# Crossbar transposes from chunk 12 on, later loads held behind them, and the third tile's attention moved under the first G2 tile

## The chip, the cores and the metric

One NeuronCore of a Trainium2 chip. The metric is the device time of one execution in microseconds (us). "Span" is the time from the first to the last instruction in the profile; it is some 1.7 us shorter than the time.

## The reference

Retention attention (a causal product with decay in place of a softmax) over q, k, v of 8 x 8 heads x 576 x 64, and then an expert layer with Mish over the 4608 tokens that come out:

```python
scores = scale * np.matmul(q, k.transpose(0, 1, 3, 2))
Dmat = np.where(rel >= 0, gamma[:, None, None] ** rel[None, :, :], 0.0)
attn = np.matmul(scores * Dmat[None], v)                      # [8, 8, 576, 64]
x = attn.transpose(0, 2, 1, 3).reshape(4608, 512)
h = x @ w_in                                                  # w_in 512 x 2048
g = h * np.tanh(softplus(h))                                  # Mish
out = g @ w_out                                               # w_out 2048 x 512
```

## The kernel before

The 4608 tokens are 36 chunks of 128. Four chunks are a tile of the expert layer (9 tiles); two chunks are a pair, the unit of loading. The names that the profile uses: `qks` is q and k of a pair after scaling by the decay (DVE), `qkT` the same transposed, `sc` the scores in PSUM, `hp` the product with w_in (G1), `gT` its Mish (ACT), `ops` the product with w_out (G2). PE works through one list of instructions in order: G1 and G2 blocks of four 128x512 matmuls (0.865 us each), with the attention of later chunks in between.

How a chunk or pair is transposed before the change:

```python
    NPE = 16
    def step_t(n):
        m, u = divmod(n, 2)
        r = pairs[m]
        # ... (cut: allocate r["qk"], the tile qkT)
        if n >= NPE:                       # from pair 8 on: the DMA crossbar
            nc.sync.dma_start_transpose(out=r["qk"]..., in_=r["qks"]...)
            return
        tp = ps_sc.tile([P, 4, NP, P], BF16, name="sc")[:, 0:2]
        for i in range(2):                 # q, then k: eight transposes by TensorE
            flat = r["qks"][:, i, u].rearrange("p h d -> p (h d)")
            for p in range(NP):
                nc.tensor.transpose(tp[:, i, p, :], flat[:, ts(p, P)], ident)
        if n < 2 * NCH:                    # chunks 4 to 7: two copies, after all eight
            nc.scalar.copy(r["qk"][:, 0, u], tp[:, 0])
            nc.vector.tensor_copy(r["qk"][:, 1, u], tp[:, 1])
        else:
            nc.scalar.copy(r["qk"][:, :, u], tp)
```

How loads are released. A crossbar transpose is issued on SP. GpSimd (POOL) issues the loads; its one-element copy of `qkT` makes it stand until the transpose has landed, and only then come its next loads. A load of a pair is three DMAs: q and k (512 KB each) and v (256 KB written, cast to bf16).

```python
    def cross(m):
        step_t(2 * m)
        nc.gpsimd.tensor_copy(seen, pairs[m]["qk"][0:1, 0, 0, 0, 0:1])

    # ... visit(m, 0) of pairs 4 to 6: load(m + 4), not held by anything
    #     pair 8:                      cross(8); load(11)
    #     m = 8 to 16:                 cross(m + 1); load(m + 4)
```

## Time and profile before

| kernel before | |
|---|---|
| time, median of 3 runs | 317.3 us (317.11 to 317.51) |
| span of the profiled run, granted clock | 315.3 us, 1.0 |
| PE busy | 304.6 us, 97% of the span |
| matmuls, of them in the chunk 12 to 15 transposes | 2635, 32 |
| crossbar transposes | 10, pairs 8 to 17 |
| G2 of the first tile starts | 57.71 us |
| scores of pair 8 / pair 9 start | 112.81 / 128.47 us |

The table is read from the top down: if PE is busy 97% of the span at the full clock, a change can win only by matmuls taken off PE or by waits of PE that go; and it can lose by any wait that it adds, since PE takes its list in order. The prediction below shows the rows behind this. One more line, from the list of DMA issues (count, median us from issue to landing):

```profile
qkT<-qks SPq DMA_TRANSPOSE x10, 4.4
```

### The profile page before, as it was taken

How to read it: one execution, taken by the hardware profiler on the slowest of the kernel's cores; microseconds unless marked ns; L12 is line 12 of the kernel's file. 1: busy time of each engine (PE TensorE's matmuls, PEld its weight loads, DVE VectorE, ACT ScalarE, POOL GpSimd, SP SyncE). 2: the span in 40 equal slices, each digit the busy share in tenths (PEclk: the TensorE clock that was granted, in tenths of full speed). 3: DMA queues.
4: the chain of work that ended last, by engine and by line, in shares of the span. 5: the costliest groups of instructions: out<-in, count | busy, mean ns of one | idle time of the engine just before them, and what ended most of it. 6: DMA issues, size and time to landing. Idle time of an engine off the chain costs nothing.

```text
span 315.3 us, 6082 instructions
## 1 busy us (share of the span) xinstructions
PE 304.6 (97%) x2635; PEld 158.8 (50%) x2635; DVE 134.9 (43%) x182; ACT 127.2 (40%) x212; POOL 78.7 (25%) x102
## 2 busy tenths in 40 slices
PE   6889999999999999999999999999999999999995
PEld 2455588655455554444545454445454545444444
DVE  5743574247738482626262626262626232001011
ACT  5667566324355542343434343434343432333300
POOL 6586672543340223122403040320000000000000
PEclk9999999999999999999999999999999999999999
DMA  6999999999996395969595969694040401000032
GB/s 171 261 178 223 197 208 221 201 228 246 221 238 79 78 199 113 189 102 197 131 174 116 185 127 175 139 163 103 33 102 33 102 33 35 33 33 35 33 83 83
DMA packets 72474, 43.38 MB, mean 138 GB/s; under 512 B 55680, under 2 KB 63616, under 8 KB 72448
## 3 DMA queue, kind: packets, MB, share of 16 engines
q0 software_dynamic: 43952, 26.22, 56.2%
q1 hardware_dynamic: 28352, 16.65, 21.3%
q8 instruction: 20, 0.33, 0.5%
q10 hardware_dynamic: 144, 0.13, 0.1%
q14 instruction: 6, 0.05, 0.0%
HBM read 36.70 MB, written 9.44 MB: 146 GB/s over the span
## 4 chain that ended last, share of the span: by engine, by line
PE 89%; DVE 3%; SPq 2%; DMA 2%; ACT 2%; issue 1%; DVEq 0%
PE hp L385 34%; PE ops L423 33%; PE hp L423 6%; PE hp L408 4%; PE sc L321 3%; PE sc L370 2%; PE sc L363 2%; SPq L137 2%; PE st L342 2%; DMA kraw<-in_k_dram 2%; PE sc L296 1%; PE hp L435 1%; DVE sm L324 1%; PE hp L396 1%; ACT qkT L298 0%
## 5 line engine op out<-in xcount | busy, mean ns | idle before, releaser
L385 PE MATMUL hp<-xT,w_in_t 128*128 128x512 bf16 x496 | 126.6, 380 | 0.7 <-ACT gT L387 0.7
L387 ACT ACTIVATE gT<-hp 128x512 bf16<-128x512 f32 x124 | 74.2, 599 | 128.5 <-PE hp L385 128.3
L423 PE MATMUL ops<-w_out_t,gT 128*128 128x512 bf16 x480 | 121.9, 379 | 0.2 <-DVE res L443 0.2
L423 PEld LDWEIGHTS <-gT 128*128 128x128 bf16 x560 | 54.2, 98 | 65.1 <-issue 1.3
L443 DVE COPY res<-ops 128x512 f32<-128x512 f32 x30 | 20.8, 692 | 129.0 <-PE ops L423 129.0
L385 PEld LDWEIGHTS <-w_in_t 128*128 128x128 bf16 x496 | 46.0, 98 | 53.8 <-issue 1.2
L324 DVE TENSOR_TENSOR sm<-sc,mask 128x1024 bf16<-128x1024 f32 x36 | 42.7, 1218 | 13.9 <-PE sc L321 13.9
L568 POOL COPY seen<-qkT 1x1 bf16<-1x1 bf16 x10 | 1.8, 178 | 128.2 <-DMA qkT<-qks 128.2
L346 ACT ACTIVATE ssb<-st,diag 128x512 bf16<-128x512 f32 x32 | 20.3, 685 | 15.5 <-PE st L342 15.5
L374 DVE CAST xT<-sc 128x512 bf16<-128x512 f32 x32 | 20.8, 686 | 6.7 <-PE sc L370 5.8
L107 POOL DMA_DIRECT2D qraw<-in_q_dram x16 | 17.2, 1074 | 13.1 <-DVE qks L280 7.5
L280 DVE TENSOR_TENSOR qks<-kraw,gk 128x1024 bf16<-128x1024 f32 (+1 forms) x18 | 19.8, 1102 | 0.0
L280 DVE TENSOR_TENSOR qks<-qraw,gq 128x1024 bf16<-128x1024 f32 (+1 forms) x18 | 19.8, 1098 | 0.0
L107 POOL DMA_DIRECT2D kraw<-in_k_dram x16 | 17.1, 1070 | 10.5 <-issue 4.9
L423 PE MATMUL hp<-w_out_t,gT 128*128 128x512 bf16 x80 | 18.8, 380 | 0.0
L107 POOL DMA_DIRECT2D v<-in_v_dram x16 | 17.2, 1074 | 6.2 <-DMA kraw<-in_k_dram 2.5
L408 PE MATMUL hp<-xT,w_in_t 128*128 128x128 bf16 x272 | 16.9, 219 | 0.0
L408 PEld LDWEIGHTS <-w_in_t 128*128 128x128 bf16 x272 | 15.4, 98 | 0.7 <-issue 0.2
L370 PE MATMUL sc<-sm,v 128*64 128x128 bf16 x288 | 13.8, 220 | 0.6 <-DVE sm L324 0.6
L321 PEld LDWEIGHTS <-qkT 64*128 64x128 bf16 x288 | 8.1, 94 | 9.8 <-issue 5.9
L410 ACT ACTIVATE gT<-hp 128x512 bf16<-128x512 f32 x17 | 10.2, 598 | 7.0 <-PE hp L408 6.8
L321 PE MATMUL sc<-qkT 64*128 64x128 bf16 x288 | 11.9, 218 | 1.1 <-DVE qkT L299 0.9
(75 smaller groups left out, 153.5 us busy)
## 6 DMA issues: line engine op xcount, KB each, us to landing
out_dram<-res SPq DMA_DIRECT2D x31, 256.0 KB, 3.5
qraw<-in_q_dram POOLq DMA_DIRECT2D x12, 512.0 KB, 8.1
kraw<-in_k_dram POOLq DMA_DIRECT2D x12, 512.0 KB, 9.3
v<-in_v_dram POOLq DMA_DIRECT2D x12, 256.0 KB, 9.8
qraw<-in_q_dram POOLq DMA_DIRECT2D x8, 256.0 KB, 9.4
kraw<-in_k_dram POOLq DMA_DIRECT2D x8, 256.0 KB, 9.4
w_out_t<-in_moe_w_out_dram POOLq DMA_DIRECT2D x4, 512.0 KB, 11.6
w_in_t<-in_moe_w_in_dram POOLq DMA_DIRECT2D x6, 256.0 KB, 7.1
```

The costliest lines, as they stand in the source:

```text
L107: nc.gpsimd.dma_start(out=r[x][ds(off, ni)].rearrange("p u h d -> p (u h) d"), in_=src[ds(b, 2), :, ds(i0, ni), :].rearrange("b h p d -> p ...
L280: nc.vector.tensor_tensor(r["qks"][:, i, u], r["qk"[i]][:, u], g, op=OP.mult)
L321: nc.tensor.matmul(sc[:, e, p, :], lhsT=qk[r, 1, u, p, :], rhs=qk[r, 0, u, p, :], start=True, stop=True)
L324: nc.vector.tensor_tensor(sm.rearrange("p e n i -> p (e n) i"), sc.rearrange("p e n i -> p (e n) i"), (mask if len(chunks[n]) == 1 else ma ...
L346: nc.scalar.activation(ssb[:, :, :, e, :], st, AX.Copy, scale=diag[:, e:e + 1])
L370: nc.tensor.matmul(ot[ds(64 * e, 64), p, :], lhsT=vs[:, u, 2 * p + e, :], rhs=sm[:, e, p, :], start=(start and p == 0), stop=True, skip_gr ...
L374: (nc.scalar.copy if t == 0 else nc.vector.tensor_copy)(xts[t][:, :, ts(s, P)], ot)
L385: nc.tensor.matmul(hp, lhsT=w_in_t[:, c, ts(f, P)], rhs=xts[t][:, c, :], start=(c == 0), stop=(c == KC - 1))
L387: nc.scalar.activation(gts[t][:, f, :], hp, AX.Mish)
L408: nc.tensor.matmul(hp[:, j, :], lhsT=w_in_t[:, c, ts(f + j, P)], rhs=xts[t][:, c, ts(s, P)], start=(c == 0), stop=(c == KC - 1))
L423: nc.tensor.matmul(ops, lhsT=gts[t][:, f, ts(s, P)], rhs=w_out_t[:, f, :], start=(f == 0), stop=(f == nF - 1))
L443: copy(ot, ops)
```

## The change

Its intent: take the 32 transposes of chunks 12 to 15 off PE by using the crossbar from pair 6 on; hold the loads of pairs 8 to 11 until the transposes ahead of them have landed, so that the two do not meet; put the attention of the third tile (pairs 4 and 5) evenly under the first G2 tile; let the q and k copies of a chunk start earlier. The core of the diff, cut (allocation moved into `turned`, xT copies of chunks 4 to 11 moved from DVE to ACT, and the start, are left out):

```diff
-    NPE = 16
 def step_t(n):                                      # chunks 4 to 7
-        for i in range(2):
+        for i, copy in enumerate((nc.scalar.copy, nc.vector.tensor_copy)):
             for p in range(NP):
                 nc.tensor.transpose(tp[:, i, p, :], flat[:, ts(p, P)], ident)
-        nc.scalar.copy(r["qk"][:, 0, u], tp[:, 0])
-        nc.vector.tensor_copy(r["qk"][:, 1, u], tp[:, 1])
+            copy(qk[:, i, u], tp[:, i])             # between the two halves
+def turn_pair(m, i):                                # pairs 4 and 5: q half, k half
+        if "tp" not in r:
+            r["tp"] = ps_sc.tile([P, 2, 2, NP, P], BF16, name="sc")   # one tile for both
+        ... eight transposes into r["tp"][:, i], then nc.scalar.copy(qk[:, i], tp)
     # first G2 tile:  turn_pair, scores, output of pairs 4 and 5 at i = 2 ... 13
     for i in range(8):                              # second G2 tile, first half
+        elif i == 2:
+            cross(6)
+            load(8)
     for i in range(nF):                             # G1 of tile 2 with the rest of G2
+        elif i == 6:
+            cross(7)
+            load(9)
-        elif i == 11:
+        elif i == 14:
             cross(8)
+            load(10)
             load(11)
```

More of the change, by code (lines that the diff above doesn't have):

```diff
@@ L280, in step_p, with turned @@
             nc.vector.tensor_tensor(r["qks"][:, i, u], r["qk"[i]][:, u], g, op=OP.mult)
-    def step_t(n):
-        m, u = divmod(n, 2)
+    def turned(m):
         r = pairs[m]
@@ L287, in step_t, with cross @@
             r["qk"] = tr.tile([P, 2, 2, NP, P], BF16, name="qkT", bufs=3)
-        if n >= NPE:
-            nc.sync.dma_start_transpose(out=r["qk"].rearrange("p i u n t -> p (i u n) t"),
-                                        in_=r["qks"].rearrange("p i u h d -> p (i u h d)"))
-            return
-        tp = ps_sc.tile([P, 4, NP, P], BF16, name="sc")[:, 0:2]
-        for i in range(2):
+        return r["qk"]
+    def step_t(n):
+        m, u = divmod(n, 2)
+        qk = turned(m)
+        tp = ps_sc.tile([P, 4, NP, P], BF16, name="sc")
+        for i, copy in enumerate((nc.scalar.copy, nc.vector.tensor_copy)):
+            flat = pairs[m]["qks"][:, i, u].rearrange("p h d -> p (h d)")
+            for p in range(NP):
+                nc.tensor.transpose(tp[:, i, p, :], flat[:, ts(p, P)], ident)
+            copy(qk[:, i, u], tp[:, i])
+    def turn_pair(m, i):
+        r = pairs[m]
+        qk = turned(m)
+        if "tp" not in r:
+            r["tp"] = ps_sc.tile([P, 2, 2, NP, P], BF16, name="sc")
+        tp = r["tp"][:, i]
+        for u in range(2):
             flat = r["qks"][:, i, u].rearrange("p h d -> p (h d)")
             for p in range(NP):
-                nc.tensor.transpose(tp[:, i, p, :], flat[:, ts(p, P)], ident)
-        if n < 2 * NCH:
-            nc.scalar.copy(r["qk"][:, 0, u], tp[:, 0])
-            nc.vector.tensor_copy(r["qk"][:, 1, u], tp[:, 1])
-        else:
-            nc.scalar.copy(r["qk"][:, :, u], tp)
+                nc.tensor.transpose(tp[:, u, p, :], flat[:, ts(p, P)], ident)
+        nc.scalar.copy(qk[:, i], tp)
+    def cross(m):
+        r = pairs[m]
+        qk = turned(m)
+        nc.sync.dma_start_transpose(out=qk.rearrange("p i u n t -> p (i u n) t"),
+                                    in_=r["qks"].rearrange("p i u h d -> p (i u h d)"))
+        nc.gpsimd.tensor_copy(seen, qk[0:1, 0, 0, 0, 0:1])
     def step_n(m):
@@ L373, in step_o @@
             xts[t] = xp.tile([P, KC, NCH * P], BF16, name="xT")
-        (nc.scalar.copy if t == 0 else nc.vector.tensor_copy)(xts[t][:, :, ts(s, P)], ot)
+        (nc.scalar.copy if t < 3 else nc.vector.tensor_copy)(xts[t][:, :, ts(s, P)], ot)
     gts = {}
@@ L503 @@
     first(2, "O")
-    first(3, "kQK")
-    for f in range(4):
+    first(3, "kQ")
+    steps = {0: "K", 1: "S", 3: "O"}
+    for f in range(5):
         g1_some(0, f, NCH - 1)
-        first(3, {0: "S", 2: "O"}.get(f, ""))
+        first(3, steps.get(f, ""))
     g1_chunk(3, 0)
-    for i in range(4, nF):
-        if i == 5:
+    g1_chunk(3, 4, 1)
+    for i in range(5, nF):
+        if i == 6:
             step_n(0)
-        elif i == 7:
+        elif i == 8:
             step_k(0)
         elif i == 9:
+            one(4, "P")
+        elif i == 10:
             step_n(1)
-        elif i == 12:
-            one(4, "PT")
+        elif i == 11:
+            one(4, "T")
+        elif i == 13:
+            one(4, "S")
         elif i == 14:
-            one(4, "S")
             one(5, "P")
@@ L541, with scores, output @@
     load(7)
-    def visit(m, w):
-        n = 2 * m
-        if w == 0:
-            if 2 * m + 2 < NPE:
-                load(m + 4)
-        elif w == 2:
-            if m == 5:
-                step_k(1)
-            one(n, "T")
-        elif w == 3:
-            one(n + 1, "T")
-        elif w == 5:
-            one(n, "S")
-            one(n + 1, "S")
-        elif w == 7:
-            step_k(m)
-            one(n, "O")
-            one(n + 1, "O")
-            if 2 * m + 2 < NPE:
-                step_p(m + 1)
-    def cross(m):
-        step_t(2 * m)
-        nc.gpsimd.tensor_copy(seen, pairs[m]["qk"][0:1, 0, 0, 0, 0:1])
+    def scores(m):
+        one(2 * m, "S")
+        one(2 * m + 1, "S")
+    def output(m):
+        step_k(m)
+        one(2 * m, "O")
+        one(2 * m + 1, "O")
     for i in range(nF):
-        if i == 6:
+        if i == 0:
             step_p(4)
-        elif i >= 8:
-            visit(4, i % 8)
+        elif i in (2, 10):
+            turn_pair(4 + i // 8, 0)
+        elif i in (3, 11):
+            turn_pair(4 + i // 8, 1)
+        elif i in (5, 13):
+            scores(4 + i // 8)
+        elif i == 8:
+            output(4)
+            step_p(5)
+        elif i == 12:
+            step_k(1)
         g2(0, i)
     for i in range(8):
-        visit(5, i)
+        if i == 0:
+            output(5)
+            step_p(6)
+        elif i == 2:
+            cross(6)
+            load(8)
         g2(1, i)
     for i in range(nF):
-        visit(6 + i // 8, i % 8)
-        if i == 9:
+        if i == 2:
+            scores(6)
+            step_p(7)
+        elif i == 5:
+            output(6)
+        elif i == 6:
+            cross(7)
+            load(9)
+        elif i == 10:
+            scores(7)
             step_p(8)
-        elif i == 11:
+        elif i == 13:
+            output(7)
+        elif i == 14:
             cross(8)
+            load(10)
             load(11)
@@ L594 @@
             m, w = 2 * (t + 1) + i // 8, i % 8
-            n = 2 * m
             if m < n_pairs:
                 if w == 0:
-                    one(n, "S")
-                    one(n + 1, "S")
+                    scores(m)
                     if m + 1 < n_pairs:
@@ L606 @@
                 elif w == 4:
-                    step_k(m)
-                    one(n, "O")
-                    one(n + 1, "O")
+                    output(m)
             if t < nT:
```

## The prediction

> **What bounds the kernel now.** I read the page's busy table first, then the waits of PE, then the timelines of PE, ACT, DVE and SP around the parts that the change touches.
>
> ```profile
> PE 304.6 (97%) x2635; PEld 158.8 (50%) x2635; DVE 134.9 (43%) x182; ACT 127.2 (40%) x212; POOL 78.7 (25%) x102
> PEclk9999999999999999999999999999999999999999
> DMA  6999999999996395969595969694040401000032
> ```
>
> PE is busy 304.6 of 315.3 us at the full clock; nothing else is over 43%. So only two things move the end: matmuls taken off PE, and PE's idle time. The DMA row matters too: the 16 DMA engines are saturated over the first 13 slices, to about 97 us. The waits of PE name the idle time that can be had:
>
> ```profile
> PE sc L321 <- DVE qkT L299: 0.9, 3, 0.3
> PE sc L262 <- ACT qkT L265: 0.8, 1, 0.8
> PE hp L385 <- ACT gT L387: 0.7, 1, 0.7
> PE sc L363 <- DVE sm L324: 0.3, 1, 0.3
> PE ops L423 <- DVE res L443: 0.2, 1, 0.2
> ```
>
> That is 2.9 us in all; the rest of the idle time lies in the first 17 us, which the change leaves alone. The second line deserves a look: four q transposes of chunk 3, then four k transposes into the same PSUM tile, and in between ACT's copy of the q half must end. The stretch of chunk 5 and that of pair 4 (chunks 8 and 9) show what transposes cost where they do not wait so (timelines of PE, then ACT, then DVE):
>
> ```profile
> 36.94 0.61 PE L296 MATMUL sc<-ident,qks 128*128 128x128 bf16 x8
> 37.38 1.06 PE L408 MATMUL hp<-xT,w_in_t 128*128 128x128 bf16 x16
> 38.73 0.40 PE L321 MATMUL sc<-qkT 64*128 64x128 bf16 x8 [0.28 <-DVE qkT L299]
> 66.35 0.61 PE L296 MATMUL sc<-ident,qks 128*128 128x128 bf16 x8
> 66.79 1.03 PE L423 MATMUL ops<-w_out_t,gT 128*128 128x512 bf16 x4
> 67.66 0.61 PE L296 MATMUL sc<-ident,qks 128*128 128x128 bf16 x8
> ...
> 37.14 0.60 ACT L387 ACTIVATE gT<-hp 128x512 bf16<-128x512 f32 x1 [1.36 <-PE hp L385]
> 37.63 0.58 ACT L298 COPY qkT<-sc 128x512 bf16<-128x512 bf16 x1
> 67.05 1.01 ACT L301 COPY qkT<-sc 128x1024 bf16<-128x1024 bf16 x1 [8.54 <-PE sc L296]
> ...
> 38.24 0.42 DVE L299 COPY qkT<-sc 128x512 bf16<-128x512 bf16 x1 [1.00 <-ACT qkT L298]
> ```
>
> Eight transposes hold PE for 37.38 - 36.94 = 0.44 us. ACT's copy of the q half of chunk 5 starts 0.69 us after the first transpose, since a Mish of the matmuls before is still running, and ends at 1.27 us. Chunks 6 and 7 repeat this to 0.01 us.
>
> The crossbar's price, from SP's and POOL's timelines:
>
> ```profile
> 103.54 1.86 SPq L289 DMA_TRANSPOSE qkT<-qks  x1
> 107.95 0.18 POOL L568 COPY seen<-qkT 1x1 bf16<-1x1 bf16 x1 [18.06 <-DMA qkT<-qks]
> ```
>
> Issued at 103.54, landed by 107.95: 4.4 us on quiet DMA engines, no PE time, and PE uses the result only at 112.8, so it is hidden.
>
> **What the Trainium skill says.** "TensorE: Matmul & The Clock Gate", in "Wait — 56ns, not 53.3ns?", gives 55.6 ns from one warm 128-column matmul to the next; the trace agrees, 0.44 us for eight. "PSUM — Partial Sum Buffer", in "Terms", says that TensorE writing and ScalarE reading the same bank and quadrant at once is an error. The q and k halves of the new step_t are 1 KiB each and share a 2 KiB bank, so they have to be serialised; the chunk 3 wait above is such a wait in this trace. "DMA: Bandwidth & Descriptors", in "Issuing engines are not separate DMA queues", says that DMAs from all issuing engines share the 16 DMA engines and interleave. The trace agrees: output stores of 256 KB land 7.8 to 8.9 us after issue while loads saturate the engines, 2.0 us when alone.
>
> **The change part by part.** I compared the two built programs engine by engine, with the instruction that each semaphore wait stands for.
>
> *Transposes of chunks 12 to 15 go to the crossbar.* 32 matmuls fewer, four groups of 0.44 us, all in the saturated stretch: -1.8 us.
>
> *Waits that go.* The output step of chunk 4 now stands two g1 blocks behind its scores instead of one: -0.35. The scores of chunks 5 to 7 waited 0.28 to 0.30 each for DVE's copy; PE will arrive later (next part), so these go: -0.9. The 0.69 before g1 of tile 2 goes, because the attention now ends eight g2 groups earlier, and about 0.15 comes back from a PSUM buffer that a store must free: -0.55. The 0.25 behind a late store goes: -0.25. Sum -2.05.
>
> *step_t, rewritten.* The old one ran all eight transposes and then both copies. The new one runs four, then ACT's copy, then four, then DVE's copy, in one PSUM tile. In the built program the fifth transpose of each of chunks 4 to 7 waits for exactly ACT's copy of the first four. By chunk 5's numbers that copy ends at 1.27 us, the fifth transpose starts about 1.32 us after the first, and would have started at 0.22: PE stands 1.10 us. PE works in order, so nothing fills it. Four chunks: +4.4.
>
> *turn_pair.* The k half of pairs 4 and 5 waits for ACT's copy of the q half in the same tile. The copy ends 0.70 + 1.01 = 1.71 us after the first transpose, so k can start at about 1.76; PE gets there after eight transposes and a g2 group, 67.66 - 66.35 = 1.31. Two pairs of 0.45: +0.9.
>
> *Start.* g1 of block 0 fills the wait between chunk 3's q and k transposes, and a fifth block is done before chunk 3 joins. But the 128-column block that completes it is only 0.23 us long, so the next g1 meets a PSUM buffer whose Mish is not done, some 0.6 us. Walking both orders through with the durations shown I get +0.2 for the new one.
>
> *Later loads held.* Pair 8's load waits for pair 6's transpose, pair 9's for pair 7's, and those of 10 and 11 for pair 8's. PE's old waits show no loads to wait for, so this costs only where a transpose is late. Pair 6: transposed after load 7 is in, slack about 3 us. Pair 7: DVE scales it some 5.1 us after the scores of pair 6 start (0.5 + two masks 2.3 + two scalings 2.3), the transpose overlaps the end of load 8, and the scores are due 12.4 us after pair 6's: slack 1 to 2 us. Pair 8: scaled 5.1 us after the scores of pair 7, which stand only 9.8 us before its own (six g1 and three g2 groups of 0.865, output and scores 2.0). Even at 4.4 us it lands with about 0.3 us to spare, and load 9 is still running then. One transpose of this trace that met the tail of loads and a store took 5.6 us; I expect 6 to 6.5. PE then waits 1 to 2 us: +1.4, the least certain term.
>
> The xT copies of chunks 4 to 11 move from DVE to ACT (0.59 against 0.69 us); neither engine is full in that stretch, so no time.
>
> Sum: -1.8 - 2.05 + 4.4 + 0.9 + 0.2 + 1.4 = +3.05. From 317.3 this gives 320.3 us.
>
> **The rivals.** *The plain gain*: the fifth transpose does not really stand, or the time is made up by the waits behind it. Then -1.8 - 2.05 + 0.2 remains, 313.7 us. For it speaks that the change plainly aims there; against it the wait in the built program and the 0.83 us that the same pattern costs at chunk 3. *DMA contention*: the bunched loads 9, 10 and 11 delay the transposes of pairs 8 and 9. At the 8 us that stores take under saturation, pair 8 would cost 3.5 us and pair 9 up to 1 more: 323 us. Against it: load 9 is more than half done when pair 8's transpose is issued. *ACT as the new bound* in the chunk stage: a Mish of 0.60, xT and qkT copies of 0.58 each per 0.9 us block. But they fall in different blocks, and the stand of PE gives ACT time; at most 0.5 us.
>
> **Range and chances.** The four stands of step_t are the firmest term after the 1.8 us, the wait for pair 8 the loosest (0 to 3.5 us). Low end: no such wait and part of the stand made up, 316.8. High end: contention, 322.5. Faster by 2% means under 311.0, below even the plain gain: 0.01. Slower by 2% needs over 323.6: 0.05. Within 2%: 0.94.
>
> **What would show it.** Right: PE waits of about 1.1 us, four times, for ACT's qkT copy in step_t; two of about 0.45 in turn_pair; PE near 2607 matmuls and some 1.5 us less busy; 12 DMA transposes; no wait of the scores of chunks 5 to 7; one wait of 1 to 2 us of the scores of pair 8 for its transpose. Wrong: no PE wait in step_t (the plain gain), waits of several us at pairs 7, 8 and 9 (contention), or PE waiting for Mish through the chunk stage.

## The result, and the profile after

| | before | after | after - before |
|---|---|---|---|
| time, median (us) | 317.4 (317.11 to 318.74, 4 runs) | 329.25 (328.48 to 329.56, 4 runs) | +11.9 |
| ratio of fast runs | | 1.0361, 95% 1.0327 to 1.0396 | |
| span of the profiled run | 315.3 | 327.6 | +12.3 |
| G2 of the first tile starts | 57.71 | 61.62 | +3.9 |
| scores of pair 8 start | 112.81 | 117.35 | +4.5 |
| scores of pair 9 start | 128.47 | 138.35 | +9.9 |

A ratio here is the mean time of one kernel's fast runs over the mean of the other's fast runs of the same rounds, so it is not quite the ratio of the medians. The last four rows say where the loss lies: 3.9 us before the first G2 tile, 0.6 from there to pair 8, 5.3 between pair 8 and pair 9, and 2.4 after pair 9. The page of the kernel after has the rows that answer to those quoted in the prediction:

```profile
PE 306.0 (93%) x2607; PEld 158.5 (48%) x2607; DVE 130.5 (40%) x174; ACT 128.0 (39%) x217; POOL 79.5 (24%) x104
PEclk9999999999999999879999999999999999999999
DMA  6999999996599969998979797979040400000023
```

PE has 28 matmuls fewer, as it should (32 transposes gone, 4 small G1 matmuls added), and yet is busy 1.4 us longer: the clock row has an 8 and a 7, where the same work takes more time. The two costliest of PE's waits:

```profile
PE sc L337 <- DMA qkT<-qks: 8.0, 2, 5.3
PE sc L295 <- ACT qkT L296: 3.8, 4, 0.9
```

The columns after the colon are us in total, times, and the longest. L337 is the scores, L295 the transposes of step_t; two waits of 0.3 us each of turn_pair's transposes come further down. The waits on the path before (0.9 of the scores for DVE's copy, for one) are gone; in their place stand 8.0 us for crossbar transposes. One of the four step_t stands (a stand is time in which PE idles at a wait), in PE's timeline (start, us, what; idle time before it and its releaser in brackets):

```profile
31.64 0.39 PE L295 MATMUL sc<-ident,qks 128*128 128x128 bf16 x4
32.96 0.38 PE L295 MATMUL sc<-ident,qks 128*128 128x128 bf16 x4 [0.94 <-ACT qkT L296]
33.19 1.89 PE L401 MATMUL hp<-xT,w_in_t 128*128 128x512 bf16 x8
```

From the first transpose to the work behind the last one 33.19 - 31.64 = 1.55 us pass, where the kernel before needs 0.44. Now the crossbar transposes of pairs 8 and 9. SP issues them at 109.94 and at 122.61 us; POOL's copy, in POOL's timeline, runs as soon as one has landed:

```profile
117.43 0.18 POOL L317 COPY seen<-qkT 1x1 bf16<-1x1 bf16 x1 [9.33 <-DMA qkT<-qks]
138.43 0.18 POOL L317 COPY seen<-qkT 1x1 bf16<-1x1 bf16 x1 [13.40 <-DMA qkT<-qks]
```

From issue to landing pair 8's takes 7.4 us and pair 9's 15.7 us (landing at 138.30), against 4.3 to 4.4 us for those of this kernel that meet no load. The loads of pairs 10 and 11 were issued from 118.13 to 123.84 and landed from 124.08 to 139.47: pair 9's transpose stands in the middle of them. And what PE does after it:

```profile
132.05 1.03 PE L439 MATMUL ops<-w_out_t,gT 128*128 128x512 bf16 x4
138.35 1.03 PE L337 MATMUL sc<-qkT 64*128 64x128 bf16 x16 [5.28 <-DMA qkT<-qks]
139.32 1.89 PE L401 MATMUL hp<-xT,w_in_t 128*128 128x512 bf16 x4
141.00 1.91 PE L439 MATMUL ops<-w_out_t,gT 128*128 128x512 bf16 x4
142.71 1.51 PE L401 MATMUL hp<-xT,w_in_t 128*128 128x512 bf16 x4
144.05 1.03 PE L439 MATMUL ops<-w_out_t,gT 128*128 128x512 bf16 x4
```

A block of four such matmuls starts 0.865 us after the one before at the full clock; here the steps are 1.68, 1.71 and 1.34, together 2.1 us too long, and the scores themselves took 0.97 instead of 0.55. These 2.5 us are the 2.4 that the table has after pair 9, to 0.1.

**Why does a transpose take 15.7 us?** The trace keeps every DMA packet. A pair's transpose is 2048 packets of 256 B. The view of DMA packets over 128 to 131 us, and again over 134 to 137 us (queue 0 is POOL's loads, queue 1 SP's; columns: packets, MB, share of the 16 engines):

```profile
q0 software_dynamic: 171, 0.63, 97.1%
q1 hardware_dynamic: 166, 0.04, 11.6%
```

```profile
q0 software_dynamic: 1236, 0.16, 79.8%
q1 hardware_dynamic: 1236, 0.32, 79.8%
```

In the first stretch the loads are q and k, in packets of 4 KB; in the second v, in packets of 128 B. In both, the transpose gets one packet for each packet of the load: 55 per us beside q and k, 412 per us beside v, where it makes some 840 per us alone. This is what the Trainium skill says in "DMA: Bandwidth & Descriptors", "Queues, rings and completion order": an engine takes turns between its queues packet by packet. Turns of that kind favour whoever has the large packets: a 256 B packet against a 4 KB one is a sixteenth of the bytes. Two parts of the 15.7 us are not turns. The transpose's first packet came 5.3 us after its issue (1.2 us when quiet), which no run explains. And from 132 to 134 us, behind a fetch of instructions, both queues nearly stood: 329 packets of the transpose where the 412 per us above would make some 820, which is 1.2 us lost (see the last section).

### The profile page after: what moved, and what is told of

Read it like the earlier page. It is cut to its first block, busy times and chain, and to the rows that moved or that the text cites. A ratio compares the mean times of both kernels' runs of the same rounds, so it can differ in the third digit from the quotient of the medians.

```text
span 327.6 us, 6045 instructions
## 1 busy us (share of the span) xinstructions
PE 306.0 (93%) x2607; PEld 158.5 (48%) x2607; DVE 130.5 (40%) x174; ACT 128.0 (39%) x217; POOL 79.5 (24%) x104
## 4 chain that ended last, share of the span: by engine, by line
PE 82%; DMA 11%; SPq 2%; ACT 2%; DVE 1%; issue 1%; POOL 0%; ACTq 0%; POOLq 0%
PE hp L401 31%; PE ops L439 29%; DMA qkT<-qks 7%; PE hp L439 5%; PE hp L424 5%; PE sc L337 3%; DMA w_in_t<-in_moe_w_in_dram 2%; SPq L136 2%; PE sc L386 2%; PE sc L379 2%; PE st L358 2%; DMA kraw<-in_k_dram 2%; PE hp L451 1%; DVE qks L279 1%; PE sc L308 1%; ACT qkT L296 1%
## 5 line engine op out<-in xcount | busy, mean ns | idle before, releaser
L403 ACT ACTIVATE gT<-hp 128x512 bf16<-128x512 f32 x123 | 73.4, 597 | 147.3 <-PE hp L401 147.0
L337 PE MATMUL sc<-qkT 64*128 64x128 bf16 x288 | 12.3, 223 | 8.3 <-DMA qkT<-qks 8.0
L337 PEld LDWEIGHTS <-qkT 64*128 64x128 bf16 x288 | 8.4, 96 | 16.9 <-DMA qkT<-qks 9.0
L390 DVE CAST xT<-sc 128x512 bf16<-128x512 f32 x24 | 15.4, 685 | 0.9
L426 ACT ACTIVATE gT<-hp 128x512 bf16<-128x512 f32 (+1 forms) x18 | 10.3, 579 | 8.2 <-PE hp L424 7.9
```

The lines of the kernel that those rows point to most:

```text
L337: nc.tensor.matmul(sc[:, e, p, :], lhsT=qk[r, 1, u, p, :], rhs=qk[r, 0, u, p, :], start=True, stop=True)
L390: (nc.scalar.copy if t < 3 else nc.vector.tensor_copy)(xts[t][:, :, ts(s, P)], ot)
L403: nc.scalar.activation(gts[t][:, f, :], hp, AX.Mish)
```

## The experiments

All twelve gave correct results. The kernel before ran beside each on the same chip, with medians of 317.09 to 317.13 us. Each edit is against the changed kernel unless it says otherwise.

| run | what it does | expected us | measured us, median | ratio to before, 95% |
|---|---|---|---|---|
| a1 | copies of step_t after all eight | 325.7 | 324.72 | 1.0216 to 1.0301 |
| a2 | one load a transpose | 321.5 | 321.4 | 1.0089 to 1.0176 |
| a3 | pair 9's wait filled with matmuls | 326.8 | 327.13 | 1.0290 to 1.0325 |
| a4 | kernel before, step_t's copies split | 320.8 | 320.75 | 1.0098 to 1.0129 |
| b1 | a1, own tiles, loads a pair earlier | 313.5 to 315 | 318.79 | 1.0024 to 1.0084 |
| b2 | loads a pair earlier | 318.7 | 321.1 | 1.0077 to 1.0175 |
| b3 | kernel before, crossbar for pairs 6, 7, not held | 325 | 332.4 (fast runs) | 1.0391 to 1.0518 |
| b4 | v of pairs 10, 11 before q and k | 321.5 | 338.82 | 1.0647 to 1.0722 |
| c1 | new order, pairs 6, 7 on TensorE | 315.3 | 315.61 | 0.9943 to 0.9967 |
| c2 | v of pairs 10, 11 after q and k | 325 to 326.5 | 326.71 | 1.0291 to 1.0332 |
| c3 | crossbar for pair 6 only, then from 8; spread loads | 314.4 | 314.68 | 0.9915 to 0.9938 |
| c4 | the change with a1, own tiles and a2 | 316.0 | 317.75 | 0.9993 to 1.0032 |

### The stands of step_t

a1 puts the copies back behind the eight transposes; a4 does the opposite to the kernel before.

```diff
# a1, against the kernel after
         for i in range(2):
             ... four transposes
-            copy(qk[:, i, u], tp[:, i])
+        nc.scalar.copy(qk[:, 0, u], tp[:, 0])
+        nc.vector.tensor_copy(qk[:, 1, u], tp[:, 1])
# a4, against the kernel before (chunks 4 to 7)
         for i in range(2):
             ... four transposes
+            (nc.scalar.copy, nc.vector.tensor_copy)[i](r["qk"][:, i, u], tp[:, i])
-        nc.scalar.copy(r["qk"][:, 0, u], tp[:, 0])
-        nc.vector.tensor_copy(r["qk"][:, 1, u], tp[:, 1])
```

> The changed kernel with one part undone: in step_t all eight transposes of a chunk run first and the two copies after, as before. Theory (half of the loss is made of stands of PE that are worth their own length): the four waits for ACT's qkT copy go (4 x 1.10 us of delay), the scores of chunks 5 to 7 wait again for DVE's copy (3 x 0.3), nothing else moves: 329.2 - 3.5 = 325.7 us. Rival (loads 4 to 11 are DMA-bound, so an earlier PE only waits longer for the transposes of pairs 8 and 9): under 1.5 us gained, the waits for pairs 8 and 9 longer than 2.8 and 5.3 us by what was saved.

> The kernel before with one part of the change alone: in step_t of chunks 4 to 7 ACT's copy of the q half follows the four q transposes, and the four k transposes come after it in the same tile. Theory: four waits of PE of about 0.94 us (1.10 us of delay each), the three waits of 0.3 us of the scores go: 317.3 + 4.4 - 0.9 = 320.8 us. Rival (a stand in this stretch is made up for by the waits behind it): within 1 us of the kernel before.

Measured: 324.72 us for a1 (324.15 to 326.99), 4.5 under the change; 320.75 for a4, 3.6 over the kernel before. In a1's timeline of PE the eight transposes are one group again, with the G1 work 0.45 us behind their start:

```profile
30.93 0.61 PE L295 MATMUL sc<-ident,qks 128*128 128x128 bf16 x8
31.38 1.89 PE L402 MATMUL hp<-xT,w_in_t 128*128 128x512 bf16 x8
```

So the stand is of the predicted size and belongs to the position of the copy alone: it can be put in and taken out of either kernel. In a4 it costs 3.6 and not 4.4, since the waits of the scores for DVE's copy (0.9 in the kernel before) go with it. In a1 these 0.9 come back, and 3.5 was expected; the 1.0 us that it won beyond that isn't the stands'. In the profiles of the six runs with split copies in the new order (after, a2, a3, b2, b4, c2) the first G2 tile starts at 60.5 to 61.6 us, in those of the five without (a1, b1, c1, c3, c4) at 57.2 to 57.6: 3.6 us between the means. The rest of a1's gain lies, in the profiled run, behind the scores of pair 9: their wait was 3.8 us instead of 5.3, and the remainder of the span 188.1 us instead of 189.2.

### Loads beside a transpose

a2 drops load 11 from its place and from then on issues one load after each transpose.

```diff
             cross(8)
             load(10)
-            load(11)
...
                         cross(m + 1)
-                        load(m + 4)
+                        load(m + 3)
```

> The changed kernel with its loads spread: one load is released after each crossbar transpose, three pairs ahead, so load 11 no longer goes with load 10. Theory (pair 9's transpose starved beside two loads, 15.7 us from issue to landing, and the PE clock fell in the wait): pair 9's transpose meets load 10 alone, lands about 1.7 us after that load's end, near 7 to 8 us from issue; the 5.3 us wait at pair 9's scores goes, the clock stays at full and the 2.4 us of slow matmuls behind it go too: 329.2 - 7.7 = 321.5 us. Pair 8's wait of 2.8 us stays. Rival (the transpose is late for another reason, its own queue or the stores on it): it takes 12 us or more again and the time stays over 327.

Measured: 321.4 us. Pair 9's transpose takes 8.6 us instead of 15.7 and is in time; of the waits for the crossbar only pair 8's is left:

```profile
PE sc L337 <- DMA qkT<-qks: 2.7, 1, 2.7
```

Thus the loads that are in flight make the transpose late, and two of them instead of one made pair 9's wait. Taking one away wins 7.8 us, the 5.3 and the 2.4 together.

### The slow clock after the wait

a3 leaves the wait of pair 9 as it is and fills it with 18 matmuls on zeros whose result nobody uses.

```diff
                 if w == 0:
+                    if m == 9:
+                        fill = ps_o.tile([P, d_model], F32, name="ops")
+                        for _ in range(18):
+                            nc.tensor.matmul(fill, lhsT=idle[:, 0:P], rhs=idle, start=True, stop=True)
                     scores(m)
```

> The changed kernel with 18 matmuls of zeros (128x512, 0.216 us each, 3.9 us) put ahead of the scores of pair 9, where PE stood idle for 5.3 us. Their result is not used. Theory (the stand lets the clock fall, and the matmuls after it run at half speed until it is back): the wait ends when it did, the clock stays at full, the 2.4 us after it are saved: 329.2 - 2.4 = 326.8 us. Rival (the slow matmuls come of something else, as the traffic of the loads): nothing saved, 329 to 330 us, with matmuls of 512 columns still at 0.43 us apart just after the wait.

Measured: 327.13 us, 2.1 less, though nothing useful was added and the transpose still takes 15.8 us. The view of busy time by windows, over 141 to 144 us (columns: the window, its length, busy time and count of PE, PEld, DVE, ACT and POOL, then the granted clock, the DMA share and GB/s), first of the kernel after:

```profile
141.00:144.00 3.00, 3.00 (x9) 1.16 (x8) 2.63 (x3) 0.60 (x1) 1.51 (x2) 0.55 0.85 197
```

and of a3:

```profile
141.00:144.00 3.00, 3.00 (x15) 1.37 (x14) 2.78 (x3) 0.80 (x2) 0.86 (x1) 1.00 1.00 239
```

The same 3.00 us of a busy PE hold 9 matmul records at a clock of 0.55 and 15 at 1.00. So this stand of PE is paid for twice, once as idle time and once as a slow clock behind it. By the trace's clock record the granted clock is 0.5 from 136.84 to 143.67 us in the kernel after, that is for 6.83 us, which begin in the wait; behind the shorter waits of a1, a3, b1, c2 and c4 it is 0.5 for 3.41 us each time (for 6.83 again behind b4's of 2.90), and a busy PE loses half of those, 1.7 us. The Trainium skill, "TensorE: Matmul & The Clock Gate", "Part 1: The HAM clock gate", gives an idle window of about 3.4 us after which the clock halves; the 5.3 us wait here agrees, but see the last section for shorter ones.

### What slows the transpose: bytes or turns

b4 and c2 load the same bytes at the same place and only change the order of the six DMAs of pairs 10 and 11.

```diff
# both
-            load(10)
-            load(11)
# b4: v first
+            load(10, "v")
+            load(11, "v")
+            load(10, "qk")
+            load(11, "qk")
# c2: v last
+            load(10, "qk")
+            load(11, "qk")
+            fetch(10, "v")
+            fetch(11, "v")
```

> The changed kernel with the order of the loads of pairs 10 and 11 turned: v first (packets of 128 B), then q and k (packets of 4 KB); the same bytes, issued at the same place. Theory (turns packet by packet): pair 9's transpose runs beside small packets, moves some 400 packets per us and lands 6 to 8 us after its issue, so the 5.3 us wait and the 2.4 us of slow clock go: about 321.5. Rival (the bytes in flight decide): it still lands some 15 us after its issue, 329.

> The changed kernel with the loads of pairs 10 and 11 in the order q, k, q, k, then both v: same bytes, but now the small packets (128 B) run when pair 9's transpose, whose first packet comes some 5 us after its issue, has started. Turns packet by packet: about 150 packets of it pass beside the last q and k packets until 130 us, then some 410 per us beside v, so it lands near 135 instead of 138.3, the wait at pair 9 is about 2.5 us instead of 5.3, and the clock falls less: 325 to 326.5. Rival (the work in the DMA engines is served in order of arrival, the transpose ends when all loads issued before it end, whatever their order): 15 us again, 329.

b4 went the wrong way: 338.82 us, and pair 9's transpose took 26.2 us, with a wait of 13.1 us. Its premise failed first: the transpose's first packet came at 127.83 us, and the v loads with their small packets had landed by 125.72, so that it met nothing but q and k packets. And then something came that neither theory has. Over 129 to 137 us the DMA engines moved

```profile
DMA packets 425, 0.36 MB, mean 45 GB/s; under 512 B 360, under 2 KB 360, under 8 KB 425
```

45 GB/s. Of the 65 load packets of 4 KB that started in this time 23 took 2 to 3.6 us each (the others 0.3 us or so), where the kernel after moved 231 GB/s at 128 to 131 us with the same two kinds of packet, those of 4 KB at 0.3 us each. Why both queues crawl here isn't settled by any run; it stays open.

c2 is the test that b4 was meant to be. Now q and k are done by 130.9 us and the transpose then runs beside v. From 131 to 132 us:

```profile
q0 software_dynamic: 412, 0.05, 79.8%
q1 hardware_dynamic: 412, 0.11, 79.8%
```

One to one again. It landed after 14.2 us instead of 15.7 (expected: some 12.5), the wait at pair 9 was 2.65 instead of 5.3 (expected 2.5), and the time 326.71. The landing lies between what the two theories expect, the wait and the time are nearer to turns, and the packets show the turns themselves. (From 132 to 134 us both queues slowed here too, behind a fetch of instructions at 131.98: some 400 packets each in place of 820.) The clock fell for 3.41 us instead of 6.83: two of the blocks behind the wait of 2.65 us step by 1.68 and 1.46 us, and the span after pair 9 is 1.5 us longer than in the kernel before, not 2.4. So the order of the same bytes matters, but it mends only part of the delay: most of it is that two whole loads are in flight.

### The crossbar without holding loads

b3 takes the kernel before and gives pairs 6 and 7 to the crossbar, with loads 9 and 10 where they were.

```diff
-        if n >= NPE:
+        if n >= 12:
...      # visit: pairs 6 and 7 transpose at w == 0, as soon as they are scaled
+            if m >= 6:
+                one(n, "T")
```

> The kernel before with the crossbar transposes of pairs 6 and 7 instead of TensorE's, loads 9 and 10 left where they were (not held). Theory (packet by packet turns): pair 6's transpose, issued near 87 us, lands only 1 to 2 us after the loads end near 100 us, a wait of about 8 us at its scores and a slow clock after it: about 325. Rival (the transpose gets a fair share of the bandwidth): lands by 95 us, a wait of 2 us or none, about 316 to 318.

Measured: 328.97 to 333.2 us in its three fast runs, granted clock 0.973 to 0.982, slower by 4.6% and 7 us over its theory. The profiled run was a slow one (clock 0.65), so its trace isn't read here, and how the 12 to 16 us divide isn't shown. The verdict speaks against one thing, that holding loads is the mistake of the change: in the old order the same two pairs on the crossbar, with loads not held, lose more than the whole change does. c4 below, which holds them and has the same pairs on the crossbar in the new order, is at 317.75.

### Moving the loads, and what the stretch has room for

b2 issues each held load a pair earlier; b1 does that together with a1 and with a PSUM tile of its own for each half in turn_pair.

```diff
+        if i == 9:               # first G2 tile
+            load(8)
...
             cross(6)
-            load(8)
+            load(9)              # and so on: cross(7) load(10), cross(8) load(11)
# b1 also: a1, and in turn_pair
-        if "tp" not in r:
-            r["tp"] = ps_sc.tile([P, 2, 2, NP, P], BF16, name="sc")
+        tp = ps_sc.tile([P, 2, 2, NP, P], BF16, name="sc")[:, 0]
```

> The changed kernel with only the held loads one pair earlier, copies and turn_pair as in the change. Theory: both DMA waits (2.8 and 5.3 us) and the slow clock after them (2.4) go: 329.2 - 10.5 = about 318.7, and the step_t stands of 4 x 1.1 us stay. Rival: a wait of 2 to 5 us stays at some pair's scores, 322 to 325.

> The changed kernel with three edits: each tile's copies to qkT after all eight transposes (worth 4.5 us as measured when done alone), each turn_pair half in a PSUM tile of its own (2 x 0.45 = 0.9), and every held load one pair earlier, load 8 already between the eighth and the later chunks of the first G2 tile. Theory: no transpose of the crossbar runs beside a load of 4 KB packets for long, so the waits of 2.8 and 5.3 us at the scores of pairs 8 and 9 go, and with them the 2.4 us of slow clock: 329.2 - 4.5 - 0.9 - 10.5 = about 313.5 to 315, that is under the kernel before (317.1). Rival (a transpose beside a load is slow wherever the load stands, and the wait only moves to pair 7 or 8): 318 to 322, with a DMA wait of over 2 us left at a pair's scores.

b2 came to 321.1 us, between its theory and its rival, with a wait of 2.2 us left at pair 8; b1 to 318.79, and its rival was right: the waits only moved.

```profile
100.85 0.62 PE L336 MATMUL sc<-qkT 64*128 64x128 bf16 x16 [1.10 <-DMA qkT<-qks]
114.10 0.62 PE L336 MATMUL sc<-qkT 64*128 64x128 bf16 x16 [3.38 <-DMA qkT<-qks]
```

Those are pairs 7 and 8. b1's own times suggest why: loads 9, 10 and 11 start at 87.70, 101.63 and 114.82, 13.2 to 13.9 us apart. A load that meets no transpose takes 9.7 us from its first issue to its last landing (141.92 to 151.63), a quiet transpose 4.3, and 0.8 us pass from a landing to the next issue (100.80 to 101.63). One after the other they need 14.8 us, more than a pair has in this stretch, so that a transpose and a load have to overlap somewhere. Later the transposes are 15.85 us apart, and there all fit and take 4.3 us.

### Versions against the kernel before

c4 is the change with its three repairable parts repaired: a1's copies, own tiles in turn_pair, a2's loads. c1 keeps only the new order and puts pairs 6 and 7 back on TensorE, with loads not held. c3 is in between: the crossbar for pair 6, whose transpose comes when loads 0 to 7 are in, TensorE for pair 7, loads 8 and 9 together in the gap, then one load after each transpose.

```diff
# c4: a1, own tiles, and a2                        (crossbar for 6, 7, 8 ...)
# c1: a1, own tiles, and
-            cross(6)
-            load(8)
+        elif i in (2, 3):
+            turn_pair(6, i - 2)     # loads 8, 9, 10 after step_p(4), (5), (6)
-            cross(7)
-            load(9)
+        elif i in (7, 8):
+            turn_pair(7, i - 7)
# c3: c4, and
             cross(6)
             load(8)
+            load(9)
-        elif i == 6:
-            cross(7)
-            load(9)
+        elif i in (7, 8):
+            turn_pair(7, i - 7)
```

> The change with all of chunks 12 on by the crossbar as it is, but with one load after each transpose, step_t's copies after all eight and own PSUM tiles in turn_pair. From the three separate measurements: 321.4 (one load a transpose) - 4.5 (copies) - 0.9 (tiles) = about 316.0, with the wait of 2.7 us at pair 8 left. Rival (the waits only trade places: without the stands the scores come earlier and the transposes don't): 318 or more, with DMA waits of over 4 us.

> The new order of the attention alone: chunks 12 to 15 back on TensorE (turn_pair, each half in its own PSUM tile), loads 8 to 10 not held, and the copies of step_t after all eight transposes. Theory: of the prediction's sum the waits that go (-2.05) and the start (+0.2) stay, the rest is undone: 317.1 - 1.85 = about 315.3, faster than the kernel before by 0.6%, with no wait for a crossbar transpose. Rival (the order itself costs, and the loss of the change isn't all transposes and waits): 317 or more.

> Crossbar for pair 6 (quiet engines) and from pair 8 on, pair 7 on TensorE, loads 8 and 9 together after pair 6's transpose, then one load after each transpose; copies of step_t after all eight, own PSUM tiles in turn_pair. Theory: no transpose meets a load of 4 KB packets that delays it past its use, so no DMA wait over 0.5 us; 317.1 - 2.05 + 0.2 - 0.9 (pair 6's transposes off TensorE) = about 314.4. Rival (pair 8's or 9's transpose is late anyway): a DMA wait of 2 us or more, 316.5 to 318.

c1: 315.61 us (315.4 to 316.34). c3: 314.68 us (314.64 to 315.05), the fastest of all, 0.7% under the kernel before. Neither has any wait for a crossbar transpose: in c3, pair 6's takes 4.38 us and pair 8's 4.25, and pair 9's takes 8.3 but has the time. Both are within 0.3 us of what was expected, but this agreement is partly luck. Both have a1's copies, and with them the waits of the scores for DVE's copy are back, in c1's and in c3's list of waits alike:

```profile
PE sc L336 <- DVE qkT L297: 0.9, 3, 0.3
```

The expectations had counted these 0.9 us as won. Without them the sums are 316.2 and 315.3 us, and both runs came some 0.6 us below. Most of that gain lies between the first G2 tile and the scores of pair 8 (53.80 us in c1 against 55.10 before, where 0.8 was predicted); what it consists of isn't shown.

c4 is 317.75 us, level with the kernel before, and 1.7 over its sum (0.8 over, with 3.6 us for the copies in place of a1's 4.5). Its wait at pair 8 was 3.0 us where 2.7 was expected; what came on top in the profiled run was the clock:

```profile
112.23 0.62 PE L336 MATMUL sc<-qkT 64*128 64x128 bf16 x16 [2.97 <-DMA qkT<-qks]
112.78 1.17 PE L400 MATMUL hp<-xT,w_in_t 128*128 128x512 bf16 x4
113.75 1.91 PE L438 MATMUL ops<-w_out_t,gT 128*128 128x512 bf16 x4
115.45 1.78 PE L400 MATMUL hp<-xT,w_in_t 128*128 128x512 bf16 x4
```

The next block starts at 117.07, so the three behind the wait step by 0.97, 1.70 and 1.62 us, 1.7 us too long in all. c4's six runs fall into 316.1 and 316.9 at a clock of 1.00 and 317.5 to 318.4 at 0.989 to 0.995. So the crossbar as far as the change takes it wins nothing over the kernel before in the one repaired form that was run; with pair 7 left on TensorE and load 9 moved to fit, c3, it is 3.1 us better.

## Why the prediction was wrong, point by point

The predicted sum was +3.05 us; the span grew by 12.3, and the time lay beyond the high end of 322.5.

- **Transposes off PE (-1.8): right.** 2607 matmuls as predicted. c1 and c3 differ, among other things, by one such pair on PE: 315.61 and 314.68.
- **Waits that go (-2.05), start (+0.2): the waits go as predicted, their worth is shown only roughly.** None of the predicted waits is left in the profile after. c1 keeps these two terms without the 0.9 us of the scores' waits, that is -0.95, and came 1.5 under the kernel before; 0.55 of that no term accounts for. The start had a wait of 0.4 us for a load of w_in that was not foreseen; no other profile has it.
- **step_t (+4.4): right.** Four stands, 1.55 - 0.45 = 1.10 us each. Net of the 0.9 us of the scores' waits that is 3.5; a4 has +3.6, and the starts of the first G2 tile differ by 3.6. That a1's median gain of 4.5 looks like the 4.4 is chance.
- **turn_pair (+0.9): right in the trace.** The two k halves start 1.77 us after the q halves (predicted 1.76, against 1.31 without the wait). It was not run by itself; with a tile for each half (b1, c1, c3, c4) no wait of these transposes is left in the list of waits.
- **Up to the first G2 tile** these add to +3.35 predicted (+4.4 - 0.35 - 0.9 + 0.2), +3.9 measured, with the 0.4 of w_in in it; over the six profiles with this start the mean is +3.3.
- **"Later loads held": the failed step.** The prediction gave this part +1.4 us, all of it at pair 8, on the ground that a transpose under loads takes 6 to 6.5 us. Pair 8's took 7.4, and its wait was 2.76 us: a term too small by half. For pair 9 the step saw no wait in the sum, and at most 1 us in the rival, and there it failed outright: 15.7 us, a wait of 5.28. The text had listed that loads 10 and 11 are both issued behind pair 8's transpose, and did not ask when pair 9's transpose is issued beside them: at 122.61, four and a half us after the first of six DMAs. Its measure for a crowded transpose was one of 5.6 us in the kernel before, and stores at 8 us. The first was misread: it didn't meet the tail of loads, since load 12 had landed at 133.18 us and it was issued at 133.94. And a store is 128 packets of 2 KB where a transpose is 2048 of 256 B: at the 55 packets per us that q and k left, by estimate, the one takes 2.3 us and the other 37. a2 and b2 show that this placing of loads is the cause: with one load a transpose, or a pair earlier, the wait at pair 9 is gone.
- **The slow clock (+2.4): missing from the sum.** The prediction never asked what PE's clock does after a wait of several us. a3 shows it separately.

Put together: 3.05 + 1.4 (pair 8 mis-sized) + 5.3 (pair 9) + 2.4 (clock) = 12.15, and the span grew by 12.3. That it fits so well is in part luck: up to the first G2 tile it is 0.55 more than predicted, and from there to pair 8 0.4 less than these terms give. The rival named DMA contention had the right kind of cause, and its price of 323 us, itself above the stated high end of 322.5, was too low for the same reason.

## What to carry to other kernels

A transpose that costs 4.4 us on quiet DMA engines is not a 4.4 us operation: before moving work to the crossbar, add up what the loads and the transposes of one period need and compare it with the period (here 14.8 against 13.2 to 13.9 us, where the waits could only be moved about), and issue a load so that no later transpose falls among its large packets. Don't put a copy that reads a PSUM tile between two groups of matmuls that write it: with both copies behind the last of them the first G2 tile started 3.6 us earlier here, and with a tile for each group the two waits of turn_pair were gone. And count a wait of PE of 2.65 us (the shortest seen with slow blocks behind it) or more at its length plus, possibly, the slow clock behind it, 1.7 us for 3.41 us at half the clock.

## What the Trainium skill lacked or had wrong

- "DMA: Bandwidth & Descriptors", "Rules for kernel authors", says that a transpose next to ordinary DMAs needs nothing. That holds for the result, which was correct in every run; for the time it doesn't: 4.3 to 4.4 us alone, some 6 to 9 us beside one load, 15.7 beside two, 26.2 in the worst case seen (b4).
- The same page has the turns packet by packet, but not what follows: 256 B packets of a transpose beside 4 KB packets of a load get 55 packets per us, beside 128 B packets 412, alone some 840. Nor has it what loads do to the lag of a transpose's first packet, 1.2 us when quiet and 2.9 and 5.3 us for pairs 8 and 9 here.
- No page has the collapse of b4, in which a transpose and q and k loads together moved 45 GB/s for 8 us. Its cause is open.
- No page has this: in the kernel before, pair 10's transpose took 5.6 us with no load in flight, where the others took 4.2 to 4.9. A 16 KB packet of the queue of instruction fetches started 136.85 us into the span, and behind it the rate of the 16 DMA engines fell to 9 GB/s and less for 1.1 us (40 columns over 133.9 to 139.6 us):

```profile
GB/s 0 0 0 0 0 0 0 0 34 192 207 221 214 201 205 205 219 214 225 219 320 210 174 57 4 0 0 7 9 9 9 9 36 286 298 457 431 388 388 187
```

  In the kernel after, the transposes of pairs 7, 8 and 9 each had such a fetch while they were served, and 19 to 28 packets of each took over 0.5 us, up to 2; pair 10's had none, and no packet over 0.5 us. The two were only seen together; no run sets the fetch apart as the cause.
- "TensorE: Matmul & The Clock Gate" gives some 3.4 us of idleness before the clock halves. Here waits of 2.65 (c2, pair 9), 2.79 (a3, pair 8) and 2.97 us (c4) already had slow blocks behind them, and waits of 2.69 (a2) and 2.76 us (after, pair 8) had none. So between 2.65 and 2.97 us the length alone doesn't decide. The runs of one kernel differ with it: a2's two at a granted clock of 1.00 took 320.0 and 320.2 us, its two at 0.995 322.6 and 322.7.
